# W_O in joined reads and the last V in one load, with a branch hint on TensorE, in a decode step of attention plus SwiGLU

## The chip, the core and the metric

The kernel runs on one core of a Trainium2 chip. The metric is the device time of one execution in microseconds. A core has TensorE (PE; its weight loads are shown apart as PEld), VectorE (DVE), ScalarE (ACT), GpSimd (POOL) and SyncE (SP), which here issues nearly all DMA transfers; 16 DMA engines carry them. Matmul results lie in PSUM banks, everything else in SBUF, 128 partitions wide.

## The reference

Four tokens (B = 4) of width 512 are normalised once, and the result feeds an attention over a cached window and a SwiGLU block, whose outputs are added to the input:

```
xn = layernorm(x)                                     # x: [4, 1, 512]
q  = xn @ wq                                          # 32 heads of 128
k, v = last 4096 positions of the caches              # 8 KV heads, each used by 4 heads
o  = softmax(q k^T / sqrt(128)) v                     # [4, 32 * 128]
out = x + o @ wo + (silu(xn @ w_gate) * (xn @ w_up)) @ w_down
```

wo is 4096 x 512, w_gate and w_up 512 x 1792, w_down 1792 x 512, the window of each cache 4 x 8 x 4096 x 128, all in bfloat16. So 81 MB are read from memory for a few kilobytes of result.

## The kernel before

**Stages.** The 32 pairs of batch and KV head are worked on two at a time, in ND = 16 steps d. A step reads 2 MB of K (`load_k`) and 2 MB of V (`load_v`) into one of two buffers each (`KB`, `VB`). TensorE transposes K (`transposes`), VectorE copies it out of PSUM (`evac`), TensorE multiplies it with the queries (`scores`), VectorE takes a maximum, ScalarE the exponential, and TensorE multiplies with V (`pv`, in two halves, s = 0 and 1) one step later. `norm` on VectorE divides by the sums and writes `OT`: partition = position within a head, then batch, then head (with 4 columns ahead for the step before the first).

**Transfers.** SyncE issues them in an order written out by hand. W_Q goes first, then K of steps 0 and 1, W_gate and W_up, and then V and K in turn, each as soon as its buffer is free (a wait on `s_pv` for V and on `s_tr` for K). W_down follows V of step 14. The last V (step 15) waits for the products of step 14 and is read in four transfers of 512 KB by `load_v_half`: two for its lower half (semaphore `d_v[1]`) and two for its upper half (`d_vz`). W_O follows in five pieces, cut at rows `WO_CUTS = (0, 16, 26, 29, 31, 32)` of the 32 that each partition gets, each with a semaphore of its own. `load` is a helper that lets a transfer read memory in longer pieces than it writes to a partition (K, V, W_gate, W_up and W_down are read so: two partitions' worth, or four, in one piece).

**The tail.** After the loop of steps TensorE multiplies with W_gate and W_up, adds x, then does the products of the last V (`pv(1, 0, ...)`, a wait for `d_vz`, `pv(1, 1, None)`), W_down's 28 matmuls, and then W_O. W_O lies in SBUF as `(p c) n -> p c n`: partition p holds rows 32p to 32p + 31 of the matrix. The attention output in `OT` has another order, so it is brought into W_O's: four transposes into `tr_ps`, a copy to `OB` by VectorE, four matmuls with the selection matrix `rep` into `op_ps`, and a copy to `OP`. `out_rows` then multiplies `OP[:, c, :]` with row c of every partition, two matmuls a row, waiting at each cut for that piece. `spin(n)` puts n matmuls in between whose result nobody reads.

**The end.** Rows 0 to 15 are inside the block of code that each engine has; rows 16 to 31 stand behind its end, where the engines meet (line 198). Then VectorE and ScalarE each copy half of the result, and ScalarE issues the output.

GpSimd makes the constants at the start, `rep` among them, and has nothing to do later. The branch and register instructions are those of the loop alone.

Of the kernel before, what the change touches and what calls it, by code (L numbers as in the profile page):

```python
# [5 lines left out]
BF16 = mybir.dt.bfloat16  # L6
# [6 lines left out]
def bass_parallel_sum__sliding_block_cached__swiglu_ffn__decode_kernel(  # L13
# [31 lines left out]
    SN = NT * C  # L45
    WIDE = 64
    PS = SN + WIDE
    NO = HQ * Dh // 128
    SCALE = float(Dh) ** -0.5
    EPS = 1e-5  # L50
    BIG = 1e30
# [13 lines left out]
    QZ = sb("qz", [128, ND, WIDE], BF16)  # L65
    ident = sb("ident", [128, 128], BF16)
    ones = sb("ones", [128, 128], BF16)
    rep = sb("rep", [32, REP, 128], BF16)
    mkr = sb("mkr", [2, 128], BF16)
    mkc = sb("mkc", [2, C], BF16)  # L70
    I8 = sb("i8", [C, C], BF16)
# [12 lines left out]
    XnT = sb("xnT", [128, NC, 32], BF16)  # L84
    den = sb("den", [128, C], FP32)
    OT = sb("oT", [128, B, REP + HQ], BF16)
    OB = sb("oB", [32, B, Dh], BF16)
    OP = sb("oP", [128, NO, B], BF16)
    ex = sb("ex", [128, NF, B], FP32)
    guT = sb("guT", [128, NF, B], BF16)  # L90
    qT = KT[:, 0:2048].bitcast(FP32)
    gT = WQ[:, 0:NF * 64].bitcast(FP32)
    uT = WQ[:, NF * 64:NF * 128].bitcast(FP32)
    I4 = sb("i4", [B, B], FP32)
    I4w = sb("i4w", [B, 64], BF16)
    y = sb("y_sb", [B, D], BF16)
# [12 lines left out]
    mt_ps = ps_acc[0:C, 0:128]  # L109
    gate_ps = ps_kt[0][:, 0:NF * 32]  # L110
    up_ps = ps_kt[1][:, 0:NF * 32]
    tr_ps = kt_ps[2][0:32, 0:B, :]
    op_ps = ps_kt[3][:, 0:B * 32]

    def sem(name):
        return nc.alloc_semaphore(name=name)
# [3 lines left out]
    d_wu = sem("d_wu")  # L120
    d_wd = sem("d_wd")
    d_out = sem("d_out")
    WO_CUTS = (0, 16, 26, 29, 31, 32)
    d_wo = [sem("d_wo%d" % q) for q in range(len(WO_CUTS) - 1)]
    d_k = [sem("d_k%d" % s) for s in range(2)]
    d_v = [sem("d_v%d" % s) for s in range(2)]
    d_vz = sem("d_vz")
    s_const = sem("s_const")
    s_xc = sem("s_xc")
    s_ss = sem("s_ss")  # L130
# [21 lines left out]
    s_up = sem("s_up")  # L152
    s_guT = sem("s_guT")
    s_t4 = sem("s_t4")
    s_ob = sem("s_ob")
    s_pm = sem("s_pm")
    s_op = sem("s_op")
# [6 lines left out]
    wg_ap = B_w_gate.rearrange("(p c) n -> p c n", c=NC)  # L164
    wu_ap = B_w_up.rearrange("(p c) n -> p c n", c=NC)
    wd_ap = B_w_down.rearrange("(p t) n -> p t n", t=NF)
    wo_ap = A_wo.rearrange("(p c) n -> p c n", c=NO)
    ds = bass.ds

    def kv_ap(cache, d, fold):  # L170
        b0 = d % 2 * 2
        return cache[b0:b0 + 2, d // 2, Sk - W:, :].rearrange("b (q t) d -> q b (t d)", t=fold * NT)
# [16 lines left out]
    def out_rows(eng, c0, c1):  # L189
        for c in range(c0, c1):  # L190
            if c in WO_CUTS:
                eng.wait_ge(d_wo[WO_CUTS.index(c)], 16)
            for n in range(2):
                last = eng.matmul(ps_acc[64 * n:64 * n + B, 0:256], OP[:, c, :], WO[:, c, 256 * n:256 * n + 256],  # L194
                                  start=False, stop=True, skip_group_check=True)
        return last

    with nc.Block() as block:

        @block.gpsimd  # L200
        def _(eng):
            eng.memset(ident[:], 0.0)
            eng.memset(I4[:], 0.0)
            eng.memset(I8[:], 0.0)
            eng.memset(I4w[:], 0.0)
            eng.memset(rep[:], 0.0)
            eng.memset(ones[:], 1.0)
            eng.memset(mkr[:], -BIG)
            eng.memset(mkc[:], 1.0)
            eng.drain()  # L210
            eng.affine_select(I4[:], I4[:], pattern=[[-1, B]], compare_op=ALU.not_equal,
                              fill=1.0, base=0, channel_multiplier=1)
            eng.affine_select(ident[:], ident[:], pattern=[[-1, 128]], compare_op=ALU.not_equal,
                              fill=1.0, base=0, channel_multiplier=1)
            eng.affine_select(I8[:], I8[:], pattern=[[-1, C]], compare_op=ALU.not_equal,
                              fill=1.0, base=0, channel_multiplier=1)
            eng.affine_select(I4w[:], I4w[:], pattern=[[-1, 64]], compare_op=ALU.not_equal,
                              fill=1.0, base=0, channel_multiplier=1)

            eng.affine_select(rep[:], rep[:], pattern=[[1, REP], [-1, 128]], compare_op=ALU.not_equal,  # L220
                              fill=1.0, base=0, channel_multiplier=REP)

            eng.affine_select(mkr[:], mkr[:].rearrange("j (q b i) -> j q b i", b=2, i=FOLD),
                              pattern=[[0, 64 // FOLD], [-1, 2], [0, FOLD]], compare_op=ALU.not_equal,
                              fill=0.0, base=0, channel_multiplier=1)
            eng.affine_select(mkc[:], mkc[:].rearrange("j (b h) -> j b h", b=2),
                              pattern=[[-1, 2], [0, REP]], compare_op=ALU.is_equal,
                              fill=0.0, base=0, channel_multiplier=1)
            eng.memset(XnT[:].bitcast(FP32), 0.0)
            eng.memset(QZ[:].bitcast(FP32), 0.0)  # L230
            eng.drain()
            eng.engine_nop().then_inc(s_const, 1)
            eng.memset(P[:], 1.0)
            eng.memset(VB[:, HKN:].bitcast(FP32), 0.0)  # L234
            eng.drain()
            eng.engine_nop().then_inc(s_const, 1)
            eng.engine_nop().then_inc(d_v[1], 16)

        @block.sync
        def _(eng):  # L240
            def load_k(d):
                if d >= 2:
                    eng.wait_ge(s_tr, 2 * NG * (d - 1))
                load_kv(eng, KB, A_k_cache, d).then_inc(d_k[d % 2], 16)

            def load_v(d):
                eng.wait_ge(s_pv, d + 1)
                load_kv(eng, VB, A_v_cache, d).then_inc(d_v[d % 2], 16)

            def load_v_half(d, h, done):  # L250

                a = d % 2 * KVN + h * HKN
                for i in range(FOLD):
                    b = i * KVN + h * HKN
                    eng.dma_start(VB[i:128:FOLD, a:a + HKN], kv_ap(A_v_cache, d, FOLD)[:, :, b:b + HKN]).then_inc(done, 16)

            def load_wo(n):
                a, b = WO_CUTS[n], WO_CUTS[n + 1]
                eng.dma_start(WO[:, a:b, :], wo_ap[:, a:b, :]).then_inc(d_wo[n], 16)

            eng.dma_start(WQ[:], wq_ap).then_inc(d_wq, 16)

            eng.wait_ge(s_xc, 1)
            load_k(0)
            load_k(1)
            load(eng, WG[:], wg_ap, fold_rows(B_w_gate)).then_inc(d_wg, 16)
            load(eng, WU[:], wu_ap, fold_rows(B_w_up)).then_inc(d_wu, 16)
            load_v(0)
            for d in range(2, ND):
                load_k(d)  # L270
                load_v(d - 1)
            load(eng, WD[:], wd_ap, fold_rows(B_w_down)).then_inc(d_wd, 16)
            eng.wait_ge(s_pv, ND)
            load_v_half(ND - 1, 0, d_v[1])
            load_v_half(ND - 1, 1, d_vz)
            for n in range(len(d_wo)):
                load_wo(n)

# [18 lines left out]
        def _(eng):  # L297
# [72 lines left out]

            eng.wait_ge(s_t4, 1)
            eng.tensor_copy(OB[:], tr_ps).then_inc(s_ob, 1)
            eng.wait_ge(s_pm, 1)
            eng.tensor_copy(OP[:].rearrange("p c b -> p b c"), op_ps.rearrange("p (b c) -> p b c", b=B)).then_inc(s_op, 1)

        @block.tensor
        def _(eng):
            def mm(o, l, r, start=False, stop=True):
                return eng.matmul(o, l, r, start=start, stop=stop, skip_group_check=True)  # L379
# [65 lines left out]
            def spin(n):  # L445

                for _ in range(n):
                    mm(ps_S[0][:], ident[:], KB[:, 0:512], start=True)
# [21 lines left out]
            pv(0, 1, ND + 1)  # L470
            shift(1, ND + 1)

            for w, o, done, d in ((WG, gate_ps, s_gate, d_wg), (WU, up_ps, s_up, d_wu)):
                eng.wait_ge(d, 16)
                for c in range(NC):
                    for j in range(4):
                        last = mm(o[32 * j:32 * j + 32, :], XnT[:, c, :],
                                  w[:, c, 32 * NF * j:32 * NF * (j + 1)], start=(c == 0))
                last.then_inc(done, 1)
            for n in range(2):  # L480
                mm(ps_acc[64 * n:64 * n + 64, 0:256], I4w[:], X[:, 256 * n:256 * n + 256], start=True)
            pv(1, 0, (8 * ND + 16 * FOLD, ND + 1))
            eng.wait_ge(d_vz, 16 * FOLD)
            pv(1, 1, None)
            eng.wait_ge(s_guT, 1)
            eng.wait_ge(d_wd, 16)
# [4 lines left out]
            for i in range(B):  # L491
                last = eng.transpose(
                    tr_ps[:, i, :],
                    OT[:, i, REP:], ident[:])
            last.then_inc(s_t4, 1)
            spin(2)
            eng.wait_ge(s_ob, 1)
            for e in range(REP):
                last = mm(op_ps.rearrange("p (b c) -> p b c", b=B), rep[:, e, :], OB[:, :, 32 * e:32 * e + 32],
                          start=(e == 0))  # L500
            last.then_inc(s_pm, 1)
            spin(3)
            eng.wait_ge(s_op, 1)
            out_rows(eng, 0, WO_CUTS[1])
            spin(3)

# [36 lines left out]
```

## Time and profile before

| | |
|---|---|
| median of 3 runs | 195.54 us (195.34 to 196.03) |
| profiled execution | 195.45 us |
| its span, first to last instruction | 194.2 us |
| mean granted TensorE clock | 0.991 |
| busy: PE, PEld, DVE, ACT, POOL | 164.6, 141.6, 115.3, 17.0, 10.5 us |
| read from memory | 81.01 MB, 417 GB/s over the span |

The span is shorter than the time of the execution, since what lies ahead of the first and behind the last instruction isn't in it. A line of the page such as `L379` is a line of the source; many matmuls share one, since a helper issues them, and are told apart by their tiles (`ps_o<-p,vbuf` are the products with V). In a table of windows a row has the stretch, its length, busy time and number of instructions for PE, PEld, DVE, ACT and POOL, the granted clock, the mean busy share of the 16 DMA engines, and GB/s. In a timeline a row has the start, the time taken, engine, line, operation, tiles and count, and in brackets how long the engine was idle before and what ended it. A row of a DMA issue has its size and the microseconds from the issue to the landing. Queue 1 carries the data, queue 8 blocks of instructions.

### The profile page before, as it was taken

The numbers are of one execution on the slowest core, as the hardware profiler recorded it, in microseconds if no ns is written. First come the engines' busy times: TensorE is split into PE (matmuls) and PEld (weight loads), VectorE is DVE, ScalarE is ACT, GpSimd is POOL, SyncE is SP. The second block draws the span as 40 slices with busy tenths as digits, with TensorE's granted clock in tenths as the row PEclk, the third lists the DMA queues.
The fourth block names the chain that finished last, engine by engine and source line by source line (L and its number), as shares of the span: only waits on it lengthen the run. The fifth ranks groups of instructions, "written<-read, shape, count | busy, mean of one in ns | idle before, by whom it ended". The sixth has DMA issues, their size and how long they took to land. (4 is left out here: it accounts for less than half of the span.)

```text
span 194.2 us, 7760 instructions
## 1 busy us (share of the span) xinstructions
PE 164.6 (85%) x3466; PEld 141.6 (73%) x3466; DVE 115.3 (59%) x250; ACT 17.0 (9%) x27; POOL 10.5 (5%) x23
## 2 busy tenths in 40 slices
PE   0127999739999989898989898989898989898995
PEld 0112988638989888888888887888788878887752
DVE  1004858517677767676767676767676767675610
ACT  6600010100110101010101010101010101010100
POOL 8930000000000000000000000000000000000000
PEclk9999999988999999999999999999999999999999
DMA  6999998999999999999999999999999999998992
GB/s 224 425 439 432 564 393 346 425 430 439 412 432 432 432 432 432 432 432 432 432 432 432 432 432 439 432 452 432 432 432 432 432 439 432 432 472 353 437 407 107
DMA packets 3830, 81.10 MB, mean 418 GB/s; under 512 B 712, under 2 KB 848, under 8 KB 1104
## 3 DMA queue, kind: packets, MB, share of 16 engines
q1 hardware_dynamic: 3808, 81.01, 97.4%
q8 instruction: 5, 0.08, 0.2%
q10 hardware_dynamic: 16, 0.01, 0.0%
q14 instruction: 1, 0.01, 0.0%
HBM read 81.01 MB, written 0.00 MB: 417 GB/s over the span
## 5 line engine op out<-in xcount | busy, mean ns | idle before, releaser
L321 DVE COPY kT<-ps_kt 128x1024 bf16<-128x1024 bf16 x128 | 79.9, 683 | 28.0 <-PE ps_kt L407 28.0
L407 PE MATMUL ps_kt<-ident,kbuf 128*128 128x128 bf16 x1024 | 65.6, 224 | 11.2 <-DMA kbuf<-in_A_k_cache_dram 10.3
L407 PEld LDWEIGHTS ps_kt<-ident,kbuf 128*128 128x128 bf16 x1024 | 60.0, 101 | 16.5 <-issue 16.5
L379 PE MATMUL ps_o<-p,vbuf 128*128 128x64 bf16 x1120 | 38.4, 193 | 0.0
L379 PEld LDWEIGHTS ps_s<-qz,kT 128*128 128x128 bf16 x1024 | 31.4, 98 | 6.8 <-issue 3.6
L379 PEld LDWEIGHTS ps_o<-p,vbuf 128*128 128x128 bf16 x1120 | 35.2, 98 | 1.1
L379 PE MATMUL ps_s<-qz,kT 128*128 x1024 | 34.8, 192 | 1.2
L292 ACT ACTIVATE p<-ps_s 128x512 bf16<-128x512 f32 x17 | 10.2, 597 | 161.9 <-PE ps_s L379 161.9
L326 DVE TENSOR_REDUCE rm<-ps_s 128x8 bf16<-128x512 f32 x17 | 11.8, 691 | 19.9 <-PE ps_s L379 19.9
L379 PE MATMUL ps_kt<-wq_sb,xnT 128*32 128x512 bf16 x32 | 3.6, 629 | 5.5 <-DMA wq_sb<-in_A_wq_dram 5.5
L379 PE MATMUL ps_o<-p,ones 128*128 128x128 bf16 (+1 forms) x69 | 7.0, 222 | 1.6 <-DVE qz L312 1.3
L379 PE MATMUL ps_s<-mkc,mkr 2*128 2x512 bf16 x17 | 6.8, 398 | 0.0
L384 PE MATMUL ps_acc<-i,xn 4*128 4x4 f32 x4 | 0.6, 254 | 7.1 <-ACT xn L289 7.1
L379 PE MATMUL ps_s<-dg,ones 8*128 8x512 bf16 x17 | 6.5, 385 | 0.0
L379 PEld LDWEIGHTS ps_o<-p,ones 128*128 128x128 bf16 x69 | 4.5, 98 | 2.7 <-issue 2.2
L379 PEld LDWEIGHTS ps_kt<-wq_sb,xnT 128*32 128x32 bf16 x32 | 1.2, 137 | 7.1 <-issue 7.1
L309 DVE STREAM_TRANSPOSE kT<-ps_kt 128x512 f32<-128x512 f32 x2 | 1.4, 718 | 8.3 <-PE ps_kt L379 8.3
L384 PEld LDWEIGHTS ps_acc<-i,xn 4*128 4x128 f32 x4 | 0.6, 207 | 7.0 <-issue 7.0
L337 DVE TENSOR_REDUCE den<-ps_o 128x8 f32<-128x128 f32 x18 | 5.0, 275 | 1.0 <-PE ps_o L379 1.0
L234 POOL MEMSET vbuf<- 128x6144 f32 x1 | 5.2, 5222 | 0.0
L331 DVE TENSOR_REDUCE m<-ps_acc 8x1 f32<-8x128 f32 x17 | 4.6, 270 | 0.3 <-PE ps_acc L379 0.3
L341 DVE TENSOR_TENSOR oT<-ps_o,den 128x8 f32 (+1 forms) x18 | 3.0, 167 | 2.9 <-issue 2.7
(68 smaller groups left out, 50.5 us busy)
## 6 DMA issues: line engine op xcount, KB each, us to landing
kbuf<-in_A_k_cache_dram SPq DMA_DIRECT2D x16, 2048.0 KB, 12.5
vbuf<-in_A_v_cache_dram SPq DMA_DIRECT2D x15, 2048.0 KB, 11.2
wq_sb<-in_A_wq_dram SPq DMA_DIRECT2D x1, 4096.0 KB, 12.3
vbuf<-in_A_v_cache_dram SPq DMA_DIRECT2D x4, 512.0 KB, 7.8
wo_sb<-in_A_wo_dram SPq DMA_DIRECT2D x1, 2048.0 KB, 13.3
wg_sb<-in_B_w_gate_dram SPq DMA_DIRECT2D x1, 1792.0 KB, 24.1
wu_sb<-in_B_w_up_dram SPq DMA_DIRECT2D x1, 1792.0 KB, 27.5
wd_sb<-in_B_w_down_dram SPq DMA_DIRECT2D x1, 1792.0 KB, 14.9
```

The lines of the kernel that those rows point to most:

```text
L234: eng.memset(VB[:, HKN:].bitcast(FP32), 0.0)
L292: eng.activation(P[:, d % 2 * PS:d % 2 * PS + SN], ps_S[d % 2][:], ACT.Exp, scale=SCALE).then_inc(s_p, 1)
L309: eng.transpose(qT[:, 512 * n:512 * n + 512], ps_kt[n][:])
L321: eng.tensor_copy(KT[:, u * HKN + 1024 * g:u * HKN + 1024 * (g + 1)], kt_ps[g].rearrange("p a b -> p (a b)")).then_inc(s_ev, 1)
L326: eng.tensor_reduce(RM[:], ps_S[bank][:].rearrange("p (t c) -> p c t", c=C), AX.X, ALU.max).then_inc(s_rm, 1)
L331: eng.tensor_reduce(m8[:], mt_ps, AX.X, ALU.max)
L337: eng.tensor_reduce(den[:], den_ps.rearrange("p (t c) -> p c t", c=C), AX.X, ALU.add)
L341: eng.tensor_tensor(OT[:, 2 * b:2 * b + 2, ds(r * REP, REP)], O_ps.rearrange("p (j h) -> p j h", j=2), den[:].rearrange("p (j h) -> p j h" ...
L379: return eng.matmul(o, l, r, start=start, stop=stop, skip_group_check=True)
L384: last = eng.transpose(xT_ps[:, c * B:(c + 1) * B], xn[:].rearrange("b (p c) -> b c p", c=NC)[:, c, :], I4[:])
L407: last = eng.transpose(kt_ps[g][:, k, :], KB[:, a:a + 128], ident[:])
```

## The change

- The last V is read by `load_v` like the others, in one transfer with joined reads; `load_v_half` and `d_vz` go, and both halves of its products wait for the whole.
- W_O gets another layout. Rows 0 to 15 of every partition are the first 2,048 rows of the matrix, 16 to a partition; rows 16 to 23 are the next 1,024, 8 to a partition; rows 24 to 31 are the rest, one to a partition. The first two are one transfer each, the last eight one transfer each, of 128 KB, all with joined reads. The cuts are (0, 16, 24, 29, 31, 32), the eight single rows sharing three semaphores.
- In the layout of one row to a partition, `OT` is already in W_O's order, so rows 24 to 31 are multiplied from `OT` itself. For the other 24 the bringing into order becomes 8 matmuls for the first 16 rows and 16 for the next 8, instead of 4 for all, and the copy to `OP` two copies, each with a step of `s_pm` and `s_op`. The transposes and `OB` cover 24 heads instead of 32.
- The selection matrices are larger. They lie in the space of W_Q, and GpSimd makes them after the queries are done (`s_q`), with a new semaphore `s_rep`.
- The six matmuls of `spin` behind the selection and behind rows 0 to 15 go; the two ahead of the selection stay.
- TensorE gets a register that holds 0, a mark ahead of W_gate's matmuls at which a branch hint is issued, a branch behind row 15 that is always taken to the end of its code, and between them the branch that the hint tells of, which never runs.

```diff
-    WO_CUTS = (0, 16, 26, 29, 31, 32)
+    WO_CUTS = (0, 16, 24, 29, 31, 32)
...
+    RUNS = ((0, 16), (16, 8))
+    NP = 24
+    rep_all = WQ[0:NP, NF * 128:NF * 128 + NP * 128]
+    rep = [rep_all[:, 1024 * n:1024 * n + 128 * (128 // r)].rearrange("a (e m) -> a e m", m=128)
+           for n, (_, r) in enumerate(RUNS)]
...
     def out_rows(eng, c0, c1):
         for c in range(c0, c1):
             if c in WO_CUTS:
-                eng.wait_ge(d_wo[WO_CUTS.index(c)], 16)
+                n = WO_CUTS.index(c)
+                eng.wait_ge(d_wo[n], 16 if c < NP else 16 * (WO_CUTS[n + 1] - c))
             for n in range(2):
-                last = eng.matmul(ps_acc[64 * n:64 * n + B, 0:256], OP[:, c, :], WO[:, c, 256 * n:256 * n + 256],
-                                  start=False, stop=True, skip_group_check=True)
+                last = eng.matmul(ps_acc[64 * n:64 * n + B, 0:256], OP[:, c, :] if c < NP else OT[:, :, REP + c],
+                                  WO[:, c, 256 * n:256 * n + 256], start=False, stop=True, skip_group_check=True)
...
+            eng.wait_ge(s_q, 2)
+            eng.memset(rep_all.bitcast(FP32), 0.0)
+            eng.drain()
+            for (h, r), to in zip(RUNS, rep):
+                eng.affine_select(to, to, pattern=[[1, 128 // r], [-1, 128]], compare_op=ALU.not_equal,
+                                  fill=1.0, base=-128 // r * h, channel_multiplier=128 // r)
+            eng.drain()
+            eng.engine_nop().then_inc(s_rep, 1)
...
             def load_wo(n):
                 a, b = WO_CUTS[n], WO_CUTS[n + 1]
-                eng.dma_start(WO[:, a:b, :], wo_ap[:, a:b, :]).then_inc(d_wo[n], 16)
+                if a < NP:
+                    w = A_wo[128 * a:128 * b, :]
+                    load(eng, WO[:, a:b, :], w.rearrange("(p c) n -> p c n", p=128),
+                         w.rearrange("(p c) n -> p (c n)", c=32)).then_inc(d_wo[n], 16)
+                    return
+                for c in range(a, b):
+                    w = A_wo[128 * c:128 * c + 128, :]
+                    load(eng, WO[:, c, :], w, w.rearrange("(p c) n -> p (c n)", p=16)).then_inc(d_wo[n], 16)
...
-            eng.wait_ge(s_pv, ND)
-            load_v_half(ND - 1, 0, d_v[1])
-            load_v_half(ND - 1, 1, d_vz)
+            load_v(ND - 1)
...
             eng.wait_ge(s_t4, 1)
             eng.tensor_copy(OB[:], tr_ps).then_inc(s_ob, 1)
-            eng.wait_ge(s_pm, 1)
-            eng.tensor_copy(OP[:].rearrange("p c b -> p b c"), op_ps.rearrange("p (b c) -> p b c", b=B)).then_inc(s_op, 1)
+            for n, (h, r) in enumerate(RUNS):
+                eng.wait_ge(s_pm, n + 1)
+                eng.tensor_copy(OP[:, h:h + r, :].rearrange("p c b -> p b c"), op_ps[n]).then_inc(s_op, 1)
...
+            flag = eng.alloc_register("flag")
+            eng.reg_mov(flag, 0)
+            hint = eng.mark_branch_hint_location()
             for w, o, done, d in ((WG, gate_ps, s_gate, d_wg), (WU, up_ps, s_up, d_wu)):
...
-            pv(1, 0, (8 * ND + 16 * FOLD, ND + 1))
-            eng.wait_ge(d_vz, 16 * FOLD)
+            pv(1, 0, (8 * ND + 16, ND + 1))
             pv(1, 1, None)
...
             spin(2)
+            eng.wait_ge(s_rep, 1)
             eng.wait_ge(s_ob, 1)
-            for e in range(REP):
-                last = mm(op_ps.rearrange("p (b c) -> p b c", b=B), rep[:, e, :], OB[:, :, 32 * e:32 * e + 32],
-                          start=(e == 0))
-            last.then_inc(s_pm, 1)
-            spin(3)
+            for n, (h, r) in enumerate(RUNS):
+                for e in range(128 // r):
+                    last = mm(op_ps[n], rep[n][:, e, :], OB[:, :, r * e:r * e + r], start=(e == 0))
+                last.then_inc(s_pm, 1)
             eng.wait_ge(s_op, 1)
             out_rows(eng, 0, WO_CUTS[1])
-            spin(3)
+            eng.wait_ge(s_op, 2)
+
+            eng.br_lt(flag, 1, on_true="tensor_tail", on_false="tensor_never")
+            with nc.body("tensor_never", valid_engines=[mybir.EngineType.PE]):
+                eng.br_lt(flag, 1, on_true="tensor_never", on_false="tensor_tail").branch_hint(hint)
+            nc.switch_bb("tensor_tail")
```

More of the change, by code (lines that the diff above doesn't have):

```diff
@@ L67, in bass_parallel_sum__sliding_block_cached__swiglu_ffn__decode_kernel @@
     ones = sb("ones", [128, 128], BF16)
-    rep = sb("rep", [32, REP, 128], BF16)
     mkr = sb("mkr", [2, 128], BF16)
@@ L86, in bass_parallel_sum__sliding_block_cached__swiglu_ffn__decode_kernel @@
     OT = sb("oT", [128, B, REP + HQ], BF16)
-    OB = sb("oB", [32, B, Dh], BF16)
-    OP = sb("oP", [128, NO, B], BF16)
+    OB = sb("oB", [NP, B, Dh], BF16)
+    OP = sb("oP", [128, NP, B], BF16)
     ex = sb("ex", [128, NF, B], FP32)
@@ L111, in bass_parallel_sum__sliding_block_cached__swiglu_ffn__decode_kernel @@
     up_ps = ps_kt[1][:, 0:NF * 32]
-    tr_ps = kt_ps[2][0:32, 0:B, :]
-    op_ps = ps_kt[3][:, 0:B * 32]
+    tr_ps = kt_ps[2][0:NP, 0:B, :]
+    op_ps = [t[:, 0:B * r].rearrange("p (b c) -> p b c", b=B) for t, (_, r) in zip((ps_kt[3], ps_kt[1]), RUNS)]
     def sem(name):
@@ L126, in bass_parallel_sum__sliding_block_cached__swiglu_ffn__decode_kernel @@
     d_v = [sem("d_v%d" % s) for s in range(2)]
-    d_vz = sem("d_vz")
     s_const = sem("s_const")
@@ L154, in bass_parallel_sum__sliding_block_cached__swiglu_ffn__decode_kernel @@
     s_t4 = sem("s_t4")
+    s_rep = sem("s_rep")
     s_ob = sem("s_ob")
@@ L166, in bass_parallel_sum__sliding_block_cached__swiglu_ffn__decode_kernel @@
     wd_ap = B_w_down.rearrange("(p t) n -> p t n", t=NF)
-    wo_ap = A_wo.rearrange("(p c) n -> p c n", c=NO)
     ds = bass.ds
@@ L205, in _ @@
             eng.memset(I4w[:], 0.0)
-            eng.memset(rep[:], 0.0)
             eng.memset(ones[:], 1.0)
@@ L218, in _ @@
                               fill=1.0, base=0, channel_multiplier=1)
-            eng.affine_select(rep[:], rep[:], pattern=[[1, REP], [-1, 128]], compare_op=ALU.not_equal,
-                              fill=1.0, base=0, channel_multiplier=REP)
             eng.affine_select(mkr[:], mkr[:].rearrange("j (q b i) -> j q b i", b=2, i=FOLD),
@@ L248, in load_v @@
                 load_kv(eng, VB, A_v_cache, d).then_inc(d_v[d % 2], 16)
[L250 to L255, printed above, removed]
             def load_wo(n):
                 a, b = WO_CUTS[n], WO_CUTS[n + 1]
-                eng.dma_start(WO[:, a:b, :], wo_ap[:, a:b, :]).then_inc(d_wo[n], 16)
+                if a < NP:
[6 more added lines that the diff above has]
+                    load(eng, WO[:, c, :], w, w.rearrange("(p c) n -> p (c n)", p=16)).then_inc(d_wo[n], 16)
             eng.dma_start(WQ[:], wq_ap).then_inc(d_wq, 16)
@@ L493, in _ @@
                     tr_ps[:, i, :],
-                    OT[:, i, REP:], ident[:])
+                    OT[:, i, REP:REP + NP], ident[:])
             last.then_inc(s_t4, 1)
             spin(2)
+            eng.wait_ge(s_rep, 1)
             eng.wait_ge(s_ob, 1)
-            for e in range(REP):
-                last = mm(op_ps.rearrange("p (b c) -> p b c", b=B), rep[:, e, :], OB[:, :, 32 * e:32 * e + 32],
-                          start=(e == 0))
-            last.then_inc(s_pm, 1)
-            spin(3)
+            for n, (h, r) in enumerate(RUNS):
+                for e in range(128 // r):
+                    last = mm(op_ps[n], rep[n][:, e, :], OB[:, :, r * e:r * e + r], start=(e == 0))
+                last.then_inc(s_pm, 1)
             eng.wait_ge(s_op, 1)
             out_rows(eng, 0, WO_CUTS[1])
-            spin(3)
+            eng.wait_ge(s_op, 2)
[3 more added lines that the diff above has]
+            nc.switch_bb("tensor_tail")
     out_rows(nc.tensor, WO_CUTS[1], NO).then_inc(s_acc, 1)
```

## The prediction

> **What bounds the kernel now.** I read the page's DMA parts first, then windows over the steady stretch and the tail.
>
> ```profile
> span 194.2 us, 7760 instructions
> HBM read 81.01 MB, written 0.00 MB: 417 GB/s over the span
> 60.00:160.00 100.00, 92.41 (x2071) 82.93 (x2068) 68.30 (x145) 5.97 (x10) 0.00 (x0) 1.00 1.00 431
> 171.00:182.00 11.00, 10.14 (x233) 8.04 (x229) 7.03 (x19) 1.45 (x3) 0.00 (x0) 1.00 1.00 425
> 182.00:187.00 5.00, 5.00 (x99) 3.56 (x95) 2.48 (x9) 0.00 (x0) 0.00 (x0) 1.00 1.02 430
> 190.00:191.00 1.00, 0.70 (x15) 0.56 (x16) 0.00 (x0) 0.00 (x0) 0.00 (x0) 1.00 0.59 214
> 191.00:192.00 1.00, 1.00 (x22) 0.61 (x16) 0.00 (x0) 0.00 (x0) 0.00 (x0) 1.00 0.15 54
> ```
>
> The last two columns are the DMA engines' mean busy share and GB/s. From 60 to 160 us the 16 engines are never idle (1.00, 431 GB/s), and so it stays through the tail up to 187 us (1.00 and 1.02). Only after 190 us does the share fall, to 0.59 and 0.15: the 16 engines have the same bytes to move but don't finish together, and the latest needs some 1.5 us more than the earliest. A piece has landed when the latest engine has.
>
> Next the tail's issues and landings; the number behind KB is us from issue to landing.
>
> ```profile
> 162.33 0.60 SPq L178 DMA_DIRECT2D wd_sb<-in_B_w_down_dram  x1
> wd_sb<-in_B_w_down_dram SPq DMA_DIRECT2D x1, 1792.0 KB, 14.9
> 172.01 0.60 SPq L255 DMA_DIRECT2D vbuf<-in_A_v_cache_dram  x1
> vbuf<-in_A_v_cache_dram SPq DMA_DIRECT2D x1, 512.0 KB, 7.7
> 173.30 0.60 SPq L255 DMA_DIRECT2D vbuf<-in_A_v_cache_dram  x1
> vbuf<-in_A_v_cache_dram SPq DMA_DIRECT2D x1, 512.0 KB, 8.8
> 173.94 0.59 SPq L259 DMA_DIRECT2D wo_sb<-in_A_wo_dram  x1
> wo_sb<-in_A_wo_dram SPq DMA_DIRECT2D x1, 2048.0 KB, 13.3
> 176.00 0.43 SPq L259 DMA_DIRECT2D wo_sb<-in_A_wo_dram  x1
> wo_sb<-in_A_wo_dram SPq DMA_DIRECT2D x1, 128.0 KB, 16.1
> 191.84 0.09 PEld L194 LDWEIGHTS ps_acc<-wo_sb,oP 128*4 128x4 bf16 x4 [0.23 <-DMA wo_sb<-in_A_wo_dram]
> 192.16 0.08 PEld L194 LDWEIGHTS ps_acc<-wo_sb,oP 128*4 128x4 bf16 x2 [0.23 <-DMA wo_sb<-in_A_wo_dram]
> ```
>
> W_down lands at 162.33 + 14.9 = 177.2, the last V's lower half at 172.01 + 7.7 = 179.7 and its upper half at 173.30 + 8.8 = 182.1, W_O's first 16 rows at 173.94 + 13.3 = 187.2 and its last row at 176.00 + 16.1 = 192.1. TensorE takes that last row at 192.16. Everything behind it (two matmuls, two copies, the output) lasts 194.2 - 192.1 = 2.1 us and is not touched. So the tail is the stream, and the change is worth what it does to the last landing. The profiled execution took 195.45 us, its span 194.2; 1.25 us lie around the span. The median of the three runs, 195.54, is 0.09 above it.
>
> **The change part by part.** Bytes stay the same, so each transfer is set against the stream's rate: 2,048 KB are 2.097 MB, at 431 GB/s 4.87 us.
>
> *V as one load.* Its four quarters took 182.1 - 177.2 = 4.9 us, the rate itself. One load can save 0 to 0.05; I take 0.05.
>
> *W_O's first 16 rows as joined reads.* They took 187.2 - 182.1 = 5.1 us, 0.25 over the rate. Either the reads of 16 KB are slower than joined ones, and the change gains 0.25, or something else took it. One thing else is there:
>
> ```profile
> q8 instruction: 1, 0.02, 3.1%
> 173.94 2.49 SPq L259 DMA_DIRECT2D wo_sb<-in_A_wo_dram  x5
> 23.43 0.55 SPq L178 DMA_DIRECT2D vbuf<-in_A_v_cache_dram  x1
> vbuf<-in_A_v_cache_dram SPq DMA_DIRECT2D x1, 2048.0 KB, 13.8
> 27.00 0.55 SPq L178 DMA_DIRECT2D kbuf<-in_A_k_cache_dram  x1
> kbuf<-in_A_k_cache_dram SPq DMA_DIRECT2D x1, 2048.0 KB, 15.3
> q8 instruction: 1, 0.02, 2.9%
> ```
>
> The first row is queue 8 between 182 and 184 us: a block of code is fetched, in 3.1% of 16 x 2 us = 1.0 us of one data engine. The last is the same between 40 and 42 us (2.9%). There K's load, whose reads are joined already, landed 27.00 + 15.3 = 42.3, 5.1 us behind V's 23.43 + 13.8 = 37.2. So a fetch alone explains the 0.25, and a block of code has to come in any case. I count the joined reads at nothing, with 0.25 as the bound of the gain.
>
> [...]
>
> *Rows 16 to 31: one piece of 8, then eight of one row.* Before, rows 16 to 31 took 192.1 - 187.2 = 4.9 us, for which the rate gives 4.87. The single row took 192.16 - 191.84 = 0.32 where 131 KB need 0.304. Eight at that price cost 8 x 0.016 = 0.13 over the rate; six of these eight rows lay in small pieces before too. Joined reads of 8 KB may take that away. Bounds -0.05 to +0.13; I take 0, nearer to the joined loads.
>
> *SP's issues.* Four V issues and five of W_O (2.49 us) become one and ten: 0.55 + 0.6 + 9 x 0.43 = 5.0 us against 4 x 0.6 + 2.49 = 4.9. They run from 171.4 to 176.5, and the first single row is wanted after 189: hidden by the 13 us of queue ahead; without that cover it would be 0.1.
>
> *TensorE.* V's lower half is no longer seen at 179.7; the products wait for the whole, at 182.1. The chain behind them:
>
> ```profile
> 181.42 0.40 PE L379 MATMUL ps_o<-p,ones 128*128 128x128 bf16 x4
> 181.65 2.03 PE L379 MATMUL ps_o<-p,vbuf 128*128 128x64 bf16 x64
> 185.56 0.41 DVE L372 COPY oB<-ps_kt 32x512 bf16<-32x512 bf16 x1 [1.03 <-PE ps_kt L492]
> 186.03 0.39 PE L379 MATMUL ps_kt<-oB,rep 32*128 32x128 bf16 x4
> 186.46 0.44 DVE L374 CAST oP<-ps_kt 128x128 bf16<-128x128 f32 x1 [0.49 <-PE ps_kt L379]
> 187.36 1.91 PE L194 MATMUL ps_acc<-wo_sb,oP 128*4 128x256 bf16 x32 [0.19 <-DMA wo_sb<-in_A_wo_dram]
> 189.21 0.82 PE L379 MATMUL ps_s<-kbuf,ident 128*128 128x512 bf16 x3
> 190.33 0.27 PE L194 MATMUL ps_acc<-wo_sb,oP 128*4 128x256 bf16 x2 [0.30 <-PEq L198]
> ```
>
> It starts 0.7 us later (182.1 for 181.42), and queued behind that wait stand W_down's matmuls, the transposes and everything of W_O. oB is ready at 185.97 + 0.7 = 186.7. Then 24 small matmuls for 4: at the 2.03/64 = 0.032 us of the V products 0.77 us, so to 187.5. The first half of oP, 64 columns where 128 took 0.44 us, runs beside the last 16 of them and is ready by 187.5 too. Rows 0 to 15 take 1.91: to 189.5. The six matmuls of filler are gone; the end of the code block costs 0.30 as before (190.03 to 190.33), so rows 16 to 23 run from 189.8 to 190.7. They land at 187.2 + 2.4 = 189.6, in time. Rows 24 to 28 land at 189.6 + 1.5 = 191.1: there TensorE waits again, 0.4 us ahead of the stream. So 1.1 us of added chain fit under the stream, and the whole of it costs 0; without this cover it would come to 0.7 + 0.4.
>
> *The filler's other use.* The trace shows what a long gap does to TensorE's clock, the last column but two:
>
> ```profile
> 40.00:42.00 2.00, 0.00 (x0) 0.00 (x0) 0.24 (x1) 0.00 (x0) 0.00 (x0) 1.00 1.18 487
> 42.00:44.00 2.00, 1.55 (x15) 1.55 (x16) 0.48 (x1) 0.00 (x0) 0.00 (x0) 0.54 1.10 475
> ```
>
> After more than 2 us without work it is granted 0.54. The gaps that the change opens are 0.7 us (at 181.4) and 0.4 (at 190.7), so I count nothing; at half the clock the last eight rows' 16 matmuls would need another 0.06 us each, 1 us, less the 0.4 of cover.
>
> *Hint, branch, GpSimd.* The trace shows no hint; its own time falls into the 0.7 us in which TensorE now waits for V. If it keeps a code fetch off a loaded DMA engine, it gains at most the same 0.25 of the late landing, not counted twice. The new selection matrix is made by GpSimd from about 18 us on and wanted at 186.7; SyncE's queue is past none of it.
>
> Sum on the last landing: -0.05 - 0 + 0 = -0.05, with ends -0.05 - 0.25 - 0.05 = -0.35 and +0.13. 195.45 - 0.05 = 195.40, and as the median stands 0.09 above, between 195.4 and 195.5: I say 195.4.
>
> **The rivals.** About 0.3% (0.59 us) is what a measurement of this kernel can tell from no change.
>
> *A fetch on a late engine (slower).* Twenty more small matmuls and six filler ones fewer, two instructions each, with the register, hint and branch instructions make TensorE's code ahead of the block's end longer by some 30 instructions, so the fetch that now falls at 190 us, when many engines are done, moves ahead, to about 188.
>
> ```profile
> q8 instruction: 1, 0.02, 5.8%
> ```
>
> This is queue 8 between 190 and 191 us: 5.8% of 16 us, 0.93 us of one engine, and no landing behind it is late (192.1). Ahead of 189 every engine still has data. If the fetch, hint or no hint, falls to one of the late engines, its last row comes 0.93 us later, 196.3; on an early one it vanishes in the 1.5 us of spread. It decides from the point where that engine's lead is under 0.35 (0.93 - 0.59). For it: the moved code; against it: the hint, and that both fetches of the tail found a place with little cost. 0.17.
>
> *TensorE's chain becomes the bound (slower).* If the hint or the always taken branch makes its sequencer wait for code, 1 us as queue 8's packets take, 0.4 of it is covered and 0.6 comes out: 196.0. It decides from a slip of 0.4. [...] 0.08.
>
> *The removed fetch and the joined reads gain together (faster).* The bound is -0.35; for more, the fetch must cost more in the timed runs than in the profile: 0.93 us if it falls to a late engine there now. Then 194.6. The spread of the three runs, 195.34 to 196.03, leaves room. 0.20.
>
> *The change does nothing to the stream, only moves work:* that is the forecast, 195.4, with 0.55.
>
> **How the numbers follow.** Forecast 0.55, all within 0.3% (its own range 195.1 to 195.7, the ends of the sum). Slower: 0.17 + 0.08 = 0.25. Faster 0.20. The range reaches from 194.6, the faster case, to 196.3, the slower ones, and leaves out of each a part.
>
> **What would show it.** Right: the DMA share stays near 1.00 to 189 us; V lands whole near 182.1; rows 0 to 15 start near 187.5; single rows land some 0.3 us apart; the last near 192.1; TensorE waits for W_O ahead of its last rows. Wrong: queue 8 shows a fetch after 184 us with a landing 0.5 to 1 us late behind it; or TensorE's last rows run without a DMA wait; or single rows land 0.4 us or more apart; or the last one lands before 191.5.

## The result, and the profile after

| | before | after |
|---|---|---|
| median | 195.56 us (22 runs, 195.32 to 197.91) | 196.81 us (22 runs, 196.38 to 198.8) |
| profiled execution | 195.45 us, span 194.2 | 197.15 us, span 195.9 |

The change makes the kernel slower: 1.0061 times, 95% interval 1.0042 to 1.0079, or 1.25 us between the medians. The forecast was 195.4 with a range that ended at 196.3.

First the issues of the tail and their landings in the changed kernel, read as before: start of the issue, then us to the landing.

```profile
163.09 0.60 SPq L183 DMA_DIRECT2D wd_sb<-in_B_w_down_dram  x1
wd_sb<-in_B_w_down_dram SPq DMA_DIRECT2D x1, 1792.0 KB, 14.9
172.17 0.54 SPq L183 DMA_DIRECT2D vbuf<-in_A_v_cache_dram  x1
vbuf<-in_A_v_cache_dram SPq DMA_DIRECT2D x1, 2048.0 KB, 10.6
172.75 0.60 SPq L183 DMA_DIRECT2D wo_sb<-in_A_wo_dram  x1
wo_sb<-in_A_wo_dram SPq DMA_DIRECT2D x1, 2048.0 KB, 14.9
173.39 0.60 SPq L183 DMA_DIRECT2D wo_sb<-in_A_wo_dram  x1
wo_sb<-in_A_wo_dram SPq DMA_DIRECT2D x1, 1024.0 KB, 18.0
178.45 0.59 SPq L183 DMA_DIRECT2D wo_sb<-in_A_wo_dram  x1
wo_sb<-in_A_wo_dram SPq DMA_DIRECT2D x1, 128.0 KB, 15.3
```

W_down lands at 178.0, V at 182.8 (4.8 later), W_O's first 16 rows at 187.6 (4.9 later). So far all runs at the stream's rate, the first 16 rows without the extra 0.25 of before. Then the piece of 8 rows lands at 191.4, 3.7 us later where 1 MB at the stream's rate takes 2.4, and the last row at 193.75. Rows 16 to 31 take 6.1 us, where they took 4.9.

W_down already lands 0.8 us later than before (177.2). That is this execution's own: in the eleven kernels below, which issue the same transfers up to there, it lands between 177.3 and 177.6. The profiled execution lies 0.34 us over its kernel's median too.

Now the windows of that stretch, with the DMA engines' busy share and GB/s last:

```profile
188.00:189.00 1.00, 1.00 (x26) 0.77 (x24) 0.52 (x2) 0.00 (x0) 0.00 (x0) 1.00 1.04 320
189.00:190.00 1.00, 1.00 (x24) 0.80 (x18) 0.00 (x0) 0.00 (x0) 0.00 (x0) 1.00 0.91 221
190.00:191.00 1.00, 0.26 (x6) 0.00 (x0) 0.00 (x0) 0.00 (x0) 0.00 (x0) 1.00 0.96 262
191.00:192.00 1.00, 0.61 (x12) 0.50 (x14) 0.00 (x0) 0.00 (x0) 0.00 (x0) 1.00 0.47 156
192.00:193.00 1.00, 0.55 (x12) 0.22 (x10) 0.00 (x0) 0.00 (x0) 0.00 (x0) 1.00 0.23 90
```

From 189 to 191 us the engines are as busy as ever (0.91 and 0.96) and move 221 and 262 GB/s; in the steady stretch of before, a share of 1.00 moved 431. They aren't short of work, their work is slow. TensorE, in the timeline, waits for it, last for the single rows (L200; matmuls and weight loads with `oT` are rows 24 to 31):

```profile
182.86 0.40 PE L389 MATMUL ps_o<-p,ones 128*128 128x128 bf16 x4 [0.64 <-DMA vbuf<-in_A_v_cache_dram]
188.35 1.91 PE L200 MATMUL ps_acc<-wo_sb,oP 128*4 128x256 bf16 x32
191.39 1.04 PE L200 MATMUL ps_acc<-wo_sb,oP 128*4 128x256 bf16 x16 [1.14 <-DMA wo_sb<-in_A_wo_dram]
192.88 1.22 PE L200 MATMUL ps_acc<-wo_sb,oT 128*4 128x256 bf16 x16 [0.45 <-DMA wo_sb<-in_A_wo_dram]
193.50 0.10 PEld L200 LDWEIGHTS ps_acc<-wo_sb,oT 128*4 128x4 bf16 x4 [0.20 <-DMA wo_sb<-in_A_wo_dram]
193.81 0.09 PEld L200 LDWEIGHTS ps_acc<-wo_sb,oT 128*4 128x4 bf16 x2 [0.22 <-DMA wo_sb<-in_A_wo_dram]
```

Queue 8 carries no packet behind 184 us; over the whole execution it has four, where before it had five.

### The profile page after: what moved, and what is told of

The parts are those of the page before. It is cut to its first block, busy times and chain, and to the rows that moved or that the text cites. A ratio compares the mean times of both kernels' runs of the same rounds, so it can differ in the third digit from the quotient of the medians.

```text
span 195.9 us, 7799 instructions
## 1 busy us (share of the span) xinstructions
PE 164.4 (84%) x3479; PEld 142.3 (73%) x3480; DVE 115.8 (59%) x251; ACT 17.0 (9%) x27; POOL 13.9 (7%) x24
## 4 chain that ended last, share of the span: by engine, by line
DMA 60%; PE 34%; SPq 2%; DVE 2%; issue 2%; DVEq 0%
DMA kbuf<-in_A_k_cache_dram 45%; PE ps_kt L417 17%; DMA wo_sb<-in_A_wo_dram 8%; PE ps_s L389 8%; DMA wq_sb<-in_A_wq_dram 6%; PE ps_o L389 5%; SPq L183 2%; PE ps_kt L389 2%; PE ps_acc L389 1%; DVE kT L330 1%; PE ps_acc L200 1%; DVE kT L318 0%; DVE qz L321 0%; DVE y_sb L528 0%; DVEq L329 0%
## 5 line engine op out<-in xcount | busy, mean ns | idle before, releaser
L389 PE MATMUL ps_o<-p,vbuf 128*128 128x64 bf16 x1120 | 39.1, 195 | 0.0
L389 PEld LDWEIGHTS ps_o<-p,vbuf 128*128 128x128 bf16 x1120 | 36.0, 99 | 1.2
```

## The experiments

**The shape of the single rows' reads.** Theory A blamed the memory, theory B the joining. Two kernels tell them apart. The first reads the single rows without joining; it is called the by-row kernel from here on.

```diff
-                    load(eng, WO[:, c, :], w, w.rearrange("(p c) n -> p (c n)", p=16)).then_inc(d_wo[n], 16)
+                    eng.dma_start(WO[:, c, :], w).then_inc(d_wo[n], 16)
```

> The changed kernel, but each of the eight single rows is read in 128 pieces of 1 KB, a partition each, not in 16 joined pieces of 8 KB. Theory A (memory: 16 engines that read inside one stretch of 128 KB get in each other's way, however long their pieces are): no better than the changed kernel, 196.8 us, and the last sixteen rows still take some 6.1 us. Theory B (the joining: one read of 8 KB that is cut into eight writes of 1 KB to eight partitions is what is slow when all engines do it): the last sixteen rows take 4.9 us as in the kernel before, and the time falls by 1.2 us, to 195.6.

Measured: 195.51 us, 1.0004 times the kernel before (0.9995 to 1.0013). The slowdown is gone.

```diff
-                    load(eng, WO[:, c, :], w, w.rearrange("(p c) n -> p (c n)", p=16)).then_inc(d_wo[n], 16)
+                    far = A_k_cache[0, c - NP, 0:2560, :].rearrange("(p x) d -> p (x d)", p=16)[:, 0:4096]
+                    load(eng, WO[:, c, :], A_k_cache[0, c - NP, 0:512, :].rearrange("(p x) d -> p (x d)", p=128), far).then_inc(d_wo[n], 16)
```

> The changed kernel, but the eight single rows come from 16 pieces of 8 KB that lie 40 KB apart, in the K cache (so rows 24 to 31 hold other data), joined and written as in the change. Theory A (crowding inside one stretch of 128 KB of memory): the eight pieces run at the stream's rate, 195.6 us. Theory B (a joined read cut into eight writes): as slow as the changed kernel, 196.8 us.

Measured: 196.94 us, 1.009 times (1.0071 to 1.0109). Pieces that lie 40 KB apart in memory are as slow: theory A falls, B stands. The same window of the two kernels, by-row first, shows busy engines at 376 and at 221 GB/s:

```profile
189.00:190.00 1.00, 0.70 (x16) 0.37 (x12) 0.00 (x0) 0.00 (x0) 0.00 (x0) 1.00 1.08 376
...
189.00:190.00 1.00, 0.85 (x16) 0.45 (x12) 0.00 (x0) 0.00 (x0) 0.00 (x0) 1.00 0.91 221
```

**How finely a read is cut.** One reading of B, called B1, is the number of writes that a read is cut into: the more, the slower. In three kernels the joined pieces of the last rows get another size:

```diff
-                    load(eng, WO[:, c, :], w, w.rearrange("(p c) n -> p (c n)", p=16)).then_inc(d_wo[n], 16)
+                    load(eng, WO[:, c, :], w, w.rearrange("(p c) n -> p (c n)", p=32)).then_inc(d_wo[n], 16)
```

> The changed kernel, but the single rows are read in 32 joined pieces of 4 KB, each cut into four writes of 1 KB. Theory B1 (what is slow is one read that is cut into many writes; the more, the slower): between the by-row kernel and the change, about 196.1 us, rows 16 to 31 in some 5.5 us. [...]

Measured: 195.67 us, 0.9996 times (0.9969 to 1.0023). Four writes a read cost nothing, which B1 had put halfway.

The second is the same edit with `p=64`.

> The changed kernel, but the single rows are read in 64 joined pieces of 2 KB, each cut into two writes of 1 KB, the ratio of the K and V loads. Theory B1: close to the by-row kernel, 195.6 us. [...]

Measured: 195.60 us, 0.9992 times (0.9961 to 1.0022). Two writes cost nothing either, as B1 had it. Next come eight writes again, but long ones:

```diff
-    WO_CUTS = (0, 16, 24, 29, 31, 32)
+    WO_CUTS = (0, 16, 24, 28, 32)
...
-                for c in range(a, b):
-                    w = A_wo[128 * c:128 * c + 128, :]
-                    load(eng, WO[:, c, :], w, w.rearrange("(p c) n -> p (c n)", p=16)).then_inc(d_wo[n], 16)
+                w = A_wo[128 * a:128 * b, :]
+                load(eng, WO[:, a:b, :], w.rearrange("(p c) n -> p c n", p=128),
+                     w.rearrange("(p c) n -> p (c n)", p=16)).then_inc(d_wo[n], 16)
```

> The changed kernel, but rows 24 to 31 come as two pieces of 4 rows to a partition, each in 16 joined reads of 32 KB cut into eight writes of 4 KB (so their rows lie in another order than the multiplication takes them in). Theory B1 (the number of writes a read is cut into): slow, the two pieces need over 3 us together, 196.5 us or more. [...]

Measured: 198.05 us, 1.0108 times (1.006 to 1.0155), the slowest of all. Its landings (8 rows, then the last 4):

```profile
172.88 0.60 SPq L183 DMA_DIRECT2D wo_sb<-in_A_wo_dram  x1
wo_sb<-in_A_wo_dram SPq DMA_DIRECT2D x1, 1024.0 KB, 18.9
174.15 0.59 SPq L183 DMA_DIRECT2D wo_sb<-in_A_wo_dram  x1
wo_sb<-in_A_wo_dram SPq DMA_DIRECT2D x1, 512.0 KB, 20.0
```

The piece of 8 rows, whose own reads are cut by four as in the changed kernel, lands at 191.8, 4.6 us behind the first 16 rows (187.1) where 1 MB at the stream's rate takes 2.4, and the end at 194.15. So it isn't short writes: 4 KB each, spread over eight partitions, are no better than 1 KB. And it spills onto a neighbour in the queue, as it did onto the 8 rows in the changed kernel.

**Number of writes, or stretch of partitions.** Both went together so far: eight writes were always eight partitions. Two kernels part them.

```diff
-    WO_CUTS = (0, 16, 24, 29, 31, 32)
+    WO_CUTS = (0, 16, 24, 28, 32)
...
-                for c in range(a, b):
-                    w = A_wo[128 * c:128 * c + 128, :]
-                    load(eng, WO[:, c, :], w, w.rearrange("(p c) n -> p (c n)", p=16)).then_inc(d_wo[n], 16)
+                for i in range(2):
+                    w = A_wo[128 * a + 256 * i:128 * a + 256 * i + 256, :]
+                    load(eng, WO[:, a + i:b:2, :], w.rearrange("(p c) n -> p c n", p=128),
+                         w.rearrange("(p o c) n -> p o (c n)", p=32, o=1)).then_inc(d_wo[n], 16)
```

> The changed kernel, but rows 24 to 31 come in four transfers of 256 KB: 32 joined reads of 8 KB each, cut into eight writes of 1 KB that go to four neighbouring partitions, two to each (so their rows lie in another order than the multiplication takes them in). Theory C1 (the number of writes that a read is cut into): eight, so as slow as the change, 196.8 us. Theory C2 (the number of neighbouring partitions that one read spreads over: four are fine, eight make the engines get in each other's way): 195.6 us.

Measured: 195.73 us, 1.001 times (0.9992 to 1.0028).

```diff
-    WO_CUTS = (0, 16, 24, 29, 31, 32)
+    WO_CUTS = (0, 16, 24, 28, 30, 32)
...
-                for c in range(a, b):
-                    w = A_wo[128 * c:128 * c + 128, :]
-                    load(eng, WO[:, c, :], w, w.rearrange("(p c) n -> p (c n)", p=16)).then_inc(d_wo[n], 16)
+                for c in range(a, b, 2):
+                    for i in range(2):
+                        w = A_wo[128 * (c + i):128 * (c + i) + 128, :]
+                        load(eng, WO[i:128:2, c:c + 2, :], w.rearrange("(p c) n -> p c n", c=2),
+                             w.rearrange("(p c) n -> p (c n)", p=16)).then_inc(d_wo[n], 16)
```

> The changed kernel, but rows 24 to 31 come in eight transfers of 128 KB, each of 16 joined reads of 8 KB that are cut into four writes of 2 KB to every second partition, so that a read spreads over a stretch of eight partitions (rows in another order than the multiplication takes them in). Theory C1 (number of writes): four, as in the kernel with reads of 4 KB, 195.6 us. Theory C2 (the stretch of partitions): eight, as slow as the change, 196.8 us.

Measured: 196.74 us, 1.0061 times (1.0043 to 1.0078). Both go the way of C2. The window from 189 to 190 us, eight writes into four partitions first, then four writes over a stretch of eight:

```profile
189.00:190.00 1.00, 0.85 (x16) 0.45 (x12) 0.00 (x0) 0.00 (x0) 0.00 (x0) 1.00 0.97 385
...
189.00:190.00 1.00, 0.62 (x12) 0.26 (x6) 0.00 (x0) 0.00 (x0) 0.00 (x0) 1.00 0.94 229
```

Equal reads of 8 KB, nearly equal shares of busy time, 385 against 229 GB/s. It isn't the number of writes. What counts is the stretch of partitions that one read is spread over, or something that goes with it: in all slow kernels a transfer of these rows holds 16 reads, in all fast ones 32 or more, and no run parts the two.

A cost at the end of each transfer is not it, because the reads themselves last longer. The packets from 189 to 191 us, in the changed kernel and then with eight writes into four partitions:

```profile
DMA packets 119, 0.48 MB, mean 242 GB/s; under 512 B 60, under 2 KB 60, under 8 KB 60
q1 hardware_dynamic: 119, 0.48, 93.5%
...
DMA packets 107, 0.55 MB, mean 275 GB/s; under 512 B 40, under 2 KB 40, under 8 KB 40
q1 hardware_dynamic: 107, 0.55, 69.0%
```

And in the changed kernel from 191 to 194 us:

```profile
DMA packets 77, 0.25 MB, mean 85 GB/s; under 512 B 46, under 2 KB 46, under 8 KB 46
q1 hardware_dynamic: 77, 0.25, 24.0%
```

Without the packets under 512 B these are 59, 67 and 31 reads of 8 KB. Dividing the share of 16 engines' 2 or 3 us by them, with the small packets at nothing, gives an estimate of 0.51, 0.33 and 0.37 us a read. The 59 and the 31 come in transfers of the same kind. So by this estimate a read is slow while many engines are at this work (93.5% of the 16 engines' time), and nearly as fast as the others when few are (24.0%).

**The hint.** The changed kernel without the register, the hint and the branches:

```diff
-            flag = eng.alloc_register("flag")
-            eng.reg_mov(flag, 0)
-            hint = eng.mark_branch_hint_location()
...
-            eng.br_lt(flag, 1, on_true="tensor_tail", on_false="tensor_never")
-            with nc.body("tensor_never", valid_engines=[mybir.EngineType.PE]):
-                eng.br_lt(flag, 1, on_true="tensor_never", on_false="tensor_tail").branch_hint(hint)
-            nc.switch_bb("tensor_tail")
```

> The changed kernel without the register, the hint and the two branches. Both theories: the last rows stay as slow, 196.8 us or a little more. If the hint keeps a fetch of code from the tail, queue 8 shows one more packet than the changed kernel's four, at about 188 to 190 us; it costs up to 0.9 us if its engine is a late one, nothing otherwise. If the branches cost time, 0.1 to 0.6 us less.

Measured: 196.77 us, 1.0066 times (1.0053 to 1.0079), so no different from the change. The same edit on top of the reads of 2 KB:

> The changed kernel with single rows read in 64 pieces of 2 KB, and without the register, the hint and the branches. If the hint is worth something once the single rows run at the stream's rate, this is slower than the same with the hint (195.6 us), by up to 0.9 us where the fetch behind the last block falls to a late engine; if not, 195.6 us, and queue 8 shows a fetch at 188 to 191 us that nothing waits for.

Measured: 195.60 us, 1.0003 times (0.9985 to 1.0021), the same as with the hint. Queue 8 over the whole execution, with the hint (reads of 2 KB) and without:

```profile
q8 instruction: 4, 0.07, 0.1%
...
q8 instruction: 5, 0.08, 0.2%
```

Register, hint and branches together do take a fetch out: without them queue 8 has a packet between 190 and 193 us in the first of the two kernels and one behind 184 us in the second. Which of the three does it, no run parts. It is worth nothing in either kernel.

**V in one load.** On the kernel before, the four transfers become one and the wait on `d_vz` goes:

```diff
-            eng.wait_ge(s_pv, ND)
-            load_v_half(ND - 1, 0, d_v[1])
-            load_v_half(ND - 1, 1, d_vz)
+            load_v(ND - 1)
```

> The kernel before with only the last V in one load. Both theories: V lands whole at about 182.1 us, TensorE starts its products 0.7 us later, W_O's landings stay where they were and the time is 195.5 us, within 0.1.

Measured: 195.80 us, 1.0025 times (1.0013 to 1.0038); the expectation of no change was wrong. The timeline shows why (the first row is the fillers, the second rows 16 to 31):

```profile
189.74 0.82 PE L377 MATMUL ps_s<-kbuf,ident 128*128 128x512 bf16 x3
190.85 1.91 PE L194 MATMUL ps_acc<-wo_sb,oP 128*4 128x256 bf16 x32 [0.30 <-PEq L198]
```

TensorE comes to row 16 at 190.85 instead of 190.33 and runs its 32 matmuls in one piece, without a wait for W_O: it has become the last. With the six fillers taken out as well:

> The kernel before with the last V in one load and without the six filler matmuls behind the selection and behind rows 0 to 15. If the 0.33 us that one load cost alone was TensorE's chain (V 0.8 us later, fillers of 1.3 us still in the way), the last rows wait for W_O's landings again and the time is back at 195.5 us. If it was the transfer, it stays at 195.8.

Measured: 195.41 us, 0.9974 times (0.9943 to 1.0005). The wait for W_O is back:

```profile
190.33 2.02 PE L194 MATMUL ps_acc<-wo_sb,oP 128*4 128x256 bf16 x32 [0.60 <-DMA wo_sb<-in_A_wo_dram]
```

No version beats the kernel before by more than these measurements can tell.

## Why the prediction was wrong

**The step that failed** is the term "Rows 16 to 31: one piece of 8, then eight of one row", taken at 0 with bounds -0.05 to +0.13. It measured +1.2 us (6.1 for 4.9). The bounds came from two rows: a single row read without joining (0.32 us for 0.304), and the joined loads at the full rate. But joining wasn't one thing. A joined read of K and V spreads over two partitions, one of the W_gate kind over four, and the single rows' 8 KB over eight, for which the trace of before has no row. Eight is where it breaks: reads over eight partitions are slow with four writes and with eight (196.74 and 196.81 us), reads over four fast with four and with eight (195.67 and 195.73; the number of reads in a transfer went along, as said above). Taking the joining away undoes the loss (the by-row kernel, 195.51 us). "Joined reads of 8 KB may take that away" had the sign wrong.

Why eight and not four isn't shown by any run here. What is shown is that busy engines merely move less: from 189 to 190 us 229 GB/s at a share of 0.94, against 385 at 0.97.

**The stream sets the end**: right. The output follows the last landing by 195.9 - 193.75 = 2.1 us, as before.

**V as one load, 0 to 0.05**: right for the transfer, 4.8 us in both its kernels. **The chain of TensorE fits under the stream**: right for the change. In the by-row kernel the products with V, which waited for its load, start at 182.28 and rows 0 to 15 at 187.76, 5.5 us behind (5.4 foretold). But it fits only since the fillers went: with them one load of V costs 0.33 us.

**The first 16 rows, joined, count for nothing**: right. Unjoined in the kernel with V in one load they take 4.9 us as well:

```profile
171.51 0.54 SPq L178 DMA_DIRECT2D vbuf<-in_A_v_cache_dram  x1
vbuf<-in_A_v_cache_dram SPq DMA_DIRECT2D x1, 2048.0 KB, 10.6
172.09 0.59 SPq L259 DMA_DIRECT2D wo_sb<-in_A_wo_dram  x1
wo_sb<-in_A_wo_dram SPq DMA_DIRECT2D x1, 2048.0 KB, 14.9
```

(182.1 to 187.0.) **The 0.25 was the fetch**: not shown, and the runs speak against it. The changed kernel fetches a block of code between 183 and 184 us, while these rows come in, and this kernel as many blocks over its execution as the kernel before (five packets on queue 8), yet in both the rows take 4.9 us, not 5.1. Nor was it the reads' own: the reads of 16 KB are in this kernel as they were. What this kernel changes is V's load alone, so the 0.25 went with the four quarter loads; why stays open. So the zero for the joining was right, its reason wasn't.

**The rivals.** The sign went to the slower side, 0.25, but neither rival was the cause: the changed kernel has no fetch behind 184 us, and TensorE waits for W_O. Slow single rows stood only among the signs of being wrong ("0.4 us or more apart"), with no rival and no price behind them. Even that sign looked in the wrong place: TensorE takes the last two groups of rows 0.31 us apart (193.50 and 193.81), and the loss shows in the piece of 8 rows ahead of them, which lands 1.3 us late.

## What to carry to other kernels

When a transfer reads longer pieces than it writes, keep each read within four neighbouring partitions, which was fast in all kernels here (195.60 to 195.73 us, against 196.74 to 198.05 for a stretch of eight); check how many it spans before taking the rate of other joined loads for it. A busy share near 1 with falling GB/s (here 0.91 at 221, against 1.00 at 431) showed slow transfers, not missing ones. Where filler work or an early partial load covers a wait, change them together: V in one load cost 0.33 us as long as the fillers stood, and nothing without them.

## What the runs showed that was not expected

Spread over eight partitions, joined reads run at 180 to 229 GB/s from 189 to 190 us, with busy shares of 0.86 to 0.94, against 376 to 402 in the kernels that read these rows otherwise. That held for writes of 1 KB and of 2 KB, and for data that lie together or apart; with writes of 4 KB the kernel's time was higher still, 198.05 us. A hint on a branch that never runs, with its register and branches, took one packet off queue 8 (five with 0.08 MB became four with 0.07). And in the by-row kernel SyncE needed 7.09 us for the issue of the last row, where the kernel before took 0.43; the row still landed 15.2 us after the issue began, and the kernel took 195.51 us:

```profile
176.99 7.09 SPq L270 DMA_DIRECT2D wo_sb<-in_A_wo_dram  x1
wo_sb<-in_A_wo_dram SPq DMA_DIRECT2D x1, 128.0 KB, 15.2
```
